# Writing the steps of TensorE into the program at their planned end

## The chip, the cores and the metric

The kernel runs on one core of a Trainium2 chip. The time is the device time of one execution in microseconds; of several runs the median is given. A profile is one execution with every instruction's begin and duration. Engines: PE is TensorE's matmuls, PEld its weight loads, DVE VectorE, ACT ScalarE, POOL GpSimd, SP the engine that issues the DMAs.

## What is computed

Window attention over 4 x 576 positions (8 heads of 64, each position sees itself and the 63 before it), then two feed-forward layers on the 2304 x 512 result, all in float32:

```python
def reference(**kwargs):
    attn_out = _attn_ref(**attn_kwargs)       # softmax(scale * q k^T, window of 64) v
    x = attn_out.transpose(0, 2, 1, 3).reshape(B * S, H * D)
    x = _moe_ref(x=x, **moe_kwargs)           # h = x @ w_in; g = s * relu(h)**2 + b; g @ w_out
    return _moe2_ref(x=x, **moe2_kwargs)      # h = x @ w_in; g = max(h,0) + alpha*min(h,0); g @ w_out
```

Both layers have w_in of 512 x 2048 and w_out of 2048 x 512.

## The kernel before

A matmul in full float32 precision is made of three matmuls of rounded parts (high x high, high x low, low x high), so each operand exists as a pair "h" and "l". Attention (function group) runs over five blocks of tokens, head pair by head pair; the first block is done in two groups of two head pairs each. The first two groups of hidden columns of layer 1 go straight through (hidden, project). The rest of layer 1 and layer 2 use Strassen's scheme with seven products in place of eight (hidden_pair): each call handles two hidden tiles of 128 columns and two halves of 384 tokens. In the last three groups of layer 2 the output side is done with seven products too (output).

In hidden_pair a product is six matmuls of 384 columns. Products 1, 2 go to a PSUM tile b1, products 5 and 4 to b4, and the sums that several outputs share to one tile "hb" of two PSUM banks (line 1661, 128 x 2 x 512 float32): products 6 and 3 to its first bank, product 7 to its second. Between them ACT copies partial sums from bank to bank (line 1027, in the trace always this line: ab<-h, aq<-h, ab<-ab, h<-ab), and VectorE adds the fourth part to both banks at the end (lines 1047, 1049). In the trace "hb" appears as "ab" and b1, b4 as "h"; the matmuls are line 1016. The lines are

```python
            product(7, 4, b3_, hb3, False)
            product(3, 5, b2_, hb2, False)
            copy(b4_, b3_, [hb3], [b4], 4)
            product(4, 6, b4_, b4, False)
```

(lines 1038 to 1041; b2_ is the first bank of "hb", b3_ the second). There are 39 such calls. The projections back to 512 columns are line 1507 (straight) and line 1299 (seven products); the planner puts them between products wherever they are ready. The last product 4 of the last call of output is made in two halves of 192 columns (line 1358), each with its own sum and its own DMA to the output.

Nothing of this is issued in the order of the listing. Every piece of work is a step of class Plan: ways (an engine, a planned cost in microseconds, the function that writes the instructions, a tail), the names it reads and writes, and a due time. step derives from the names which earlier steps it depends on; the two banks of "hb" are two names. emit is a list scheduler: it keeps for each engine when it is free, for each step when it is done, takes the step that can begin first (the one most due if several on that engine can), and calls its function at once. So instructions are written to the program in the order in which the planner begins them, for all engines alike, and the order of each engine is the order of its steps. The semaphore waits are made afterwards from that program: an instruction waits for those written before it on other engines that touch the same memory.

Of the kernel before, what the change touches and what calls it, by code (L numbers as in the profile page):

```python
# [2 lines left out]

# [79 lines left out]
class Plan:  # L83
# [100 lines left out]
    def emit(self):  # L184
        n = len(self.steps)
        after = [[] for _ in range(n)]
        for i, (_, deps, _, first, _) in enumerate(self.steps):
            for d in deps + first:
                after[d].append(i)
        path = [0.0] * n  # L190
        for i in range(n - 1, -1, -1):
            cost = min(w[1] + w[3] for w in self.steps[i][0])
            path[i] = cost + max((path[j] + 0.1 for j in after[i]), default=0.0)
        rank = [(-self.steps[i][2], path[i]) for i in range(n)]

        def hop(a, b):

            if a == b:
                return 0.0 if a == "pe" else 0.12
            return 0.2 if "pe" in (a, b) else 0.1  # L200

        took = {}
        left = [len(s[1]) + len(s[3]) for s in self.steps]
        done = [0.0] * n
        free = {"sp": 0.7, "dve": 2.2, "pool": 0.75, "act": 2.0, "pe": 1.1}
        pool_from = 0.0
        ready = {i for i in range(n) if left[i] == 0}
        order = []
        while ready:
            cands = []  # L210
            for i in ready:
                ways, deps, _, _, after_ = self.steps[i]
                best = None
                for w in ways:
                    share = len(w) > 4
                    w = w[:4]
                    t = max((done[d] + hop(took[d], w[0]) for d in deps), default=0.0)
                    t = max(t, free.get(w[0], 0.0), after_)
                    if w[0] == "pe" and t < self.SLOW:
                        w = (w[0], w[1] * 2, w[2], w[3])  # L220
                    if w[0] == "sp" and t < self.SLOW_DMA:
                        w = (w[0], w[1] * self.DMA_FACTOR, w[2], w[3])
                    if share:
                        w = (w[0], w[1] + 0.8 * max(0.0, min(free["pool"], t + w[1]) - max(t, pool_from)), w[2], w[3])
                    value = t + w[1] * (1.0 + self.SPARE[w[0]]) + w[3]
                    if best is None or value < best[0]:
                        best = (value, t, w)
                cands.append((best[1], i, best[2]))
            t0, i0, b0 = min(cands, key=lambda c: (c[0], self.steps[c[1]][2], c[1]))
            t0, i0, b0 = max(  # L230
                (c for c in cands if c[2][0] == b0[0] and c[0] <= t0 + self.WINDOW),
                key=lambda c: (rank[c[1]], -c[1]),
            )
            eng, cost, fn, tail = b0
            free[eng] = t0 + cost
            if eng == "pool":
                pool_from = t0
            done[i0] = t0 + cost + tail
            took[i0] = eng
            ready.remove(i0)  # L240
            order.append((t0, eng))
            fn()
            for j in after[i0]:
                left[j] -= 1
                if left[j] == 0:
                    ready.add(j)
        assert len(order) == n
        return max(done)


@with_exitstack
# [1528 lines left out]
```

## Time and profile before

| | |
|---|---|
| median of 3 runs | 842.01 us (841.2 to 842.93) |
| the profiled execution | 841.64 us |
| its span, first to last instruction | 839.6 us |
| granted TensorE clock, mean | 0.999 |
| PE busy | 821.4 us (98%) |
| PEld busy | 768.6 us (92%) |
| DVE busy | 702.6 us (84%) |
| ACT busy | 555.2 us (66%) |
| POOL busy | 105.4 us (13%) |
| DMA queue 1, share of 16 engines | 74.2% |

Busy times are unions of the instructions' spans. A row of a timeline merges neighbouring instructions of one line and kind: begin, duration of the whole run, engine, line, operation, written<-read, shapes, count; in brackets how long the engine stood idle before it and what ended that. A matmul's end is modelled and reaches over the begin of the next one, so what counts on PE is the distance between begins.

### The profile page before, as it was taken

The numbers are of one execution on the slowest core, as the hardware profiler recorded it, in microseconds if no ns is written. First come the engines' busy times: TensorE is split into PE (matmuls) and PEld (weight loads), VectorE is DVE, ScalarE is ACT, GpSimd is POOL, SyncE is SP. The second block draws the span as 40 slices with busy tenths as digits, with TensorE's granted clock in tenths as the row PEclk, the third lists the DMA queues.
The fourth block names the chain that finished last, engine by engine and source line by source line (L and its number), as shares of the span: only waits on it lengthen the run. The fifth ranks groups of instructions, "written<-read, shape, count | busy, mean of one in ns | idle before, by whom it ended". The sixth has DMA issues, their size and how long they took to land.

```text
span 839.6 us, 15049 instructions
## 1 busy us (share of the span) xinstructions
PE 821.4 (98%) x5481; PEld 768.6 (92%) x5485; DVE 702.6 (84%) x1195; ACT 555.2 (66%) x1249; POOL 105.4 (13%) x117
## 2 busy tenths in 40 slices
PE   7899999999999999999999999999999999999998
PEld 4688887888899999999999999999989999999998
DVE  6977899698995698789949898978799988888695
ACT  6777997644575576778748677775566566656461
POOL 6542355532100001001000000000000000000000
PEclk9999999999999999999999999999999999999999
DMA  8575976476648999989698676998785599469813
GB/s 284 185 231 153 283 229 197 164 261 242 236 170 324 368 342 368 405 311 369 249 388 300 259 314 246 333 363 304 278 301 187 211 328 346 131 212 350 319 47 114
DMA packets 81258, 224.61 MB, mean 268 GB/s; under 512 B 8096, under 2 KB 33824, under 8 KB 81184
## 3 DMA queue, kind: packets, MB, share of 16 engines
q1 hardware_dynamic: 81184, 223.65, 74.2%
q8 instruction: 43, 0.70, 0.3%
q14 instruction: 31, 0.25, 0.1%
HBM read 154.67 MB, written 68.94 MB: 266 GB/s over the span
## 4 chain that ended last, share of the span: by engine, by line
PE 69%; DVE 13%; DMA 12%; ACT 3%; issue 1%; POOL 1%; SPq 0%; DVEq 0%; ACTq 0%; POOLq 0%
PE y L1507 16%; PE h L1016 14%; PE y L1299 13%; PE ab L1016 11%; PE h L1417 7%; DMA raw<-w_out 4%; PE y L1477 3%; DMA raw<-w_in 3%; DMA vd<-al 2%; DVE raw L694 1%; PE ab L531 1%; PE y L636 1%; PE y L605 1%; DVE raw L699 1%; DVE raw L690 1%
## 5 line engine op out<-in xcount | busy, mean ns | idle before, releaser
L1016 PE MATMUL h<-ax,aw 128*128 128x384 f32 x936 | 184.4, 335 | 2.0 <-ACT h L1027 1.2
L1016 PEld LDWEIGHTS h<-ax,aw 128*128 128x128 f32 x936 | 163.9, 188 | 4.1 <-ACT h L1027 1.8
L1507 PE MATMUL y<-ax,woh 128*128 128x384 f32 x672 | 153.9, 335 | 2.3 <-DVE ay L1601 1.8
L1016 PE MATMUL ab<-ax,aw 128*128 128x384 f32 x702 | 139.9, 335 | 1.1 <-ACT ab L1027 0.6
L1016 PEld LDWEIGHTS ab<-ax,aw 128*128 128x128 f32 x702 | 122.9, 188 | 3.0 <-ACT ab L1027 1.6
L1507 PEld LDWEIGHTS y<-ax,woh 128*128 128x128 f32 x672 | 119.3, 188 | 4.2 <-DVE ay L1601 3.3
L1507 PE MATMUL y<-ax,wol 128*128 128x384 f32 x336 | 95.0, 334 | 0.0
L1417 PE MATMUL h<-ax,aw 128*128 128x512 f32 (+1 forms) x360 | 84.3, 377 | 0.8 <-DVE ax L654 0.7
L1417 PEld LDWEIGHTS h<-ax,aw 128*128 128x128 f32 x360 | 61.9, 189 | 12.4 <-DVE ax L654 1.6
L1299 PE MATMUL y<-ax,woh 128*128 128x384 f32 (+1 forms) x273 | 61.7, 333 | 0.0
L1507 PEld LDWEIGHTS y<-ax,wol 128*128 128x128 f32 x336 | 61.5, 188 | 0.0
L1128 ACT ACTIVATE al<-h 128x384 f32<-128x384 f32 (+2 forms) x58 | 30.1, 519 | 40.0 <-PE h L1417 21.6
L680 ACT ACTIVATE raw<-raw 128x512 f32<-128x512 f32 x56 | 37.5, 674 | 21.8 <-DMA raw<-w_in 14.2
L588 POOL TENSOR_TENSOR as__83<-as__83,den 128x512 f32<-128x512 f32 x36 | 41.5, 1173 | 59.9 <-DVE den L581 37.0
L1299 PEld LDWEIGHTS y<-ax,woh 128*128 128x128 f32 x273 | 48.4, 188 | 0.3 <-ACT y L1313 0.3
L1323 DVE TENSOR_TENSOR ay<-y,ay 128x384 f32<-128x384 f32 (+1 forms) x73 | 39.3, 546 | 10.5 <-PE y L1299 6.6
L764 POOL TENSOR_TENSOR al<-al,raw 128x512 f32<-128x512 f32 x15 | 21.8, 1450 | 193.4 <-DVE raw L699 193.4
L694 DVE SCALAR_TENSOR_TENSOR raw<-raw 128x512 int32<-128x512 int32 x56 | 42.9, 773 | 2.9 <-ACT raw L684 2.7
L1299 PE MATMUL y<-ag,wol 128*128 128x384 f32 x192 | 43.9, 335 | 0.4 <-DVE ag L711 0.4
L1313 ACT COPY y<-y 128x384 f32<-128x384 f32 x54 | 25.1, 465 | 27.7 <-PE y L1299 24.2
L1145 ACT ACTIVATE aq<-aq,slope 128x384 f32<-128x384 f32 x48 | 27.2, 610 | 23.9 <-DVE aq L1049 23.8
L570 ACT ACTIVATE as__83<-as__83,nm 128x128 f32<-128x128 f32 x96 | 37.3, 392 | 4.7 <-DVE nm L556 4.5
(189 smaller groups left out, 1670.9 us busy)
## 6 DMA issues: line engine op xcount, KB each, us to landing
ax<-xd SPq DMA_DIRECT2D x91, 768.0 KB, 6.8
aw<-wd SPq DMA_DIRECT2D x33, 512.0 KB, 5.3
xd<-ax SPq DMA_DIRECT2D x21, 768.0 KB, 4.1
raw<-w_in SPq DMA_DIRECT2D x28, 512.0 KB, 5.7
raw<-w_out SPq DMA_DIRECT2D x28, 512.0 KB, 5.6
wd<-ag SPq DMA_DIRECT2D x27, 512.0 KB, 5.0
xd<-aq SPq DMA_DIRECT2D x12, 768.0 KB, 4.2
xd<-ax SPq DMA_DIRECT2D x36, 192.0 KB, 4.7
```

Source lines behind the costliest of these rows:

```text
L570: nc.scalar.activation(sm3()[:, x, :], S_(h)[:, i * P:(i + 1) * P] if summed else sm3()[:, x, :], AF.Exp, bias=T[nm][:, x:x + 1], scale=sc ...
L588: eng.tensor_mul(x, x, d)
L680: [act(512, lambda: nc.scalar.activation(T[t], H().bitcast(F32), AF.Abs, scale=65536.0))],
L694: [dve(512, lambda: nc.vector.scalar_tensor_tensor(out=L(), in0=H(), scalar=-0x80000000, in1=L(), op0=ALU.bitwise_and, op1=ALU.bitwise_or) ...
L1016: nc.tensor.matmul(bank(), W[:, wj, a, kt * P:(kt + 1) * P], X[:, c, kt, :], start=start and kt == 0 and y == 0, stop=kt == 1 and y == 2, ...
L1128: T.step([act(n, lambda: nc.scalar.activation(rn(), hn(), AF.Relu)), dve(n, lambda: nc.vector.tensor_scalar_max(rn(), hn(), 0.0))], reads= ...
L1145: T.step([act(HALF, lambda: nc.scalar.activation(r2n(), hn(), AF.Identity, scale=slope[:, f:f + 1]))], reads=[hk, "side"], writes=[r2], at ...
L1299: nc.tensor.matmul(v(to)[:, c], W[:, s, a * P:(a + 1) * P], G[:, h, c], start=start and p == 0 and y == 0, stop=p == 1 and y == 2, skip_gr ...
L1323: [dve(e.stop - e.start, lambda: nc.vector.tensor_add(T[k][:, e], v(x)[:, e], T[k][:, e]))],
L1417: nc.tensor.matmul(T[ps][:, :n].rearrange("p (c t) -> p c t", t=P), T[w][:, k * P:(k + 1) * P], T[X(x, k)], start=st, stop=sp,)
L1477: nc.tensor.matmul(T[Y(m)][:, :n], T[w[a]][:, m * P:(m + 1) * P], T[gx[c]], start=(x == 0 and j == 0), stop=(x == len(fs) - 1 and j == 2),)
L1507: nc.tensor.matmul(ps, T[w][:, m * P:(m + 1) * P], T[x], start=(i == 0 and j == 0 and not carried(m, layer, g)), stop=(last and j == 2), s ...
```

## The change

emit no longer calls a step's function when it picks the step. It records the picks, and a new function, write, calls the functions in a second pass: a step's key is its planned begin, for a step of PE its planned begin plus its planned cost, that is its planned end. Among the steps whose dependencies are written, and whose predecessor on the same engine is written, the one with the smallest key comes next. The picks, their engines and each engine's order stay as they are; what differs is the place of PE's steps among those of the other engines.

```diff
             order.append((t0, eng))
-            fn()
+            picked.append((i0, b0))
...
+        self.write(picked, [t for t, _ in order], after)
         return max(done)
+
+    def write(self, picked, begins, after):
+
+        left = [len(s[1]) + len(s[3]) for s in self.steps]
+        then, last, way, key = {}, {}, {}, {}
+        for (i, b), t in zip(picked, begins):
+            way[i] = (t, b)
+            key[i] = t + b[1] if b[0] == "pe" else t
+            if b[0] in last:
+                then[last[b[0]]] = i
+                left[i] += 1
+            last[b[0]] = i
+        heap = [(key[i], i) for i in way if left[i] == 0]
+        heapq.heapify(heap)
+        count = 0
+        while heap:
+            _, i0 = heapq.heappop(heap)
+            t0, (eng, cost, fn, _) = way[i0]
+            count += 1
+            fn()
+            for j in after[i0] + ([then[i0]] if i0 in then else []):
+                left[j] -= 1
+                if left[j] == 0:
+                    heapq.heappush(heap, (key[j], j))
+        assert count == len(way)
```

## Rows read from the trace of the kernel before

**Rows 1.** The page's first section: busy us, share of the span, instructions.
```profile
PE 821.4 (98%) x5481; PEld 768.6 (92%) x5485; DVE 702.6 (84%) x1195; ACT 555.2 (66%) x1249; POOL 105.4 (13%) x117
```

**Rows 2.** The chain that ended last, share of the span by engine.
```profile
PE 69%; DVE 13%; DMA 12%; ACT 3%; issue 1%; POOL 1%; SPq 0%; DVEq 0%; ACTq 0%; POOLq 0%
```

**Rows 3.** Busy us of each engine from 235 us to the end.
```profile
235.00:840.00 605.00, 595.25 (x3405) 588.03 (x3403) 502.02 (x876) 388.35 (x756) 9.48 (x7) 1.00 0.78 285
```

**Rows 4.** Timeline of PE, 388 to 395 us.
```profile
388.66 1.20 PE L1016 MATMUL ab<-ax,aw 128*128 128x384 f32 x6
389.70 0.51 PE L1507 MATMUL y<-ax,woh 128*128 128x384 f32 x2
...
390.22 1.21 PE L1016 MATMUL ab<-ax,aw 128*128 128x384 f32 x6
391.98 1.31 PE L1016 MATMUL h<-ax,aw 128*128 128x384 f32 x6 [0.55 <-ACT h L1027]
393.12 0.51 PE L1507 MATMUL y<-ax,woh 128*128 128x384 f32 x2
...
394.29 0.61 PE L1507 MATMUL y<-ax,woh 128*128 128x384 f32 x2 [0.48 <-DVE ay L1601]
```

**Rows 5.** Timeline of ACT in the same stretch.
```profile
389.66 0.73 ACT L769 ACTIVATE woh<-raw,s_sb 128x512 fp32r<-128x512 f32 x1
391.46 0.46 ACT L1027 COPY h<-ab 128x384 f32<-128x384 f32 x1 [1.07 <-PE ab L1016]
```

**Rows 6.** Timelines of PE and of ACT, 437 to 443 us.
```profile
440.53 0.51 PE L1507 MATMUL y<-ax,woh 128*128 128x384 f32 x2
...
441.20 1.31 PE L1016 MATMUL ab<-ax,aw 128*128 128x384 f32 x6
...
440.67 0.48 ACT L1027 COPY h<-ab 128x384 f32<-128x384 f32 x1
```

**Rows 7.** Timelines of PE and of ACT, 372 to 377 us.
```profile
373.06 2.24 PE L1016 MATMUL ab<-ax,aw 128*128 128x384 f32 x12
...
375.33 0.46 ACT L1027 COPY h<-ab 128x384 f32<-128x384 f32 x1 [1.10 <-PE ab L1016]
```

**Rows 8.** Timeline of PE, 579 to 586 us.
```profile
580.48 2.25 PE L1016 MATMUL ab<-ax,aw 128*128 128x384 f32 x12
583.34 2.35 PE L1016 MATMUL h<-ax,aw 128*128 128x384 f32 x12 [0.61 <-ACT h L1027]
```

**Rows 9.** Timelines of PE and of ACT, 453 to 458 us.
```profile
454.35 2.24 PE L1016 MATMUL ab<-ax,aw 128*128 128x384 f32 x12
...
455.97 0.51 ACT L1500 COPY y<-ay 128x384 f32<-128x384 f32 x1
456.63 0.46 ACT L1027 COPY h<-ab 128x384 f32<-128x384 f32 x1 [0.15 <-PE ab L1016]
```

**Rows 10.** Timelines of PE and of DVE at the end, 834 to 840 us.
```profile
835.20 0.50 PE L1299 MATMUL y<-ax,woh 128*128 128x192 f32 x3
835.53 0.49 PE L1299 MATMUL y<-ax,wol 128*128 128x192 f32 x3
...
836.07 0.62 DVE L1323 TENSOR_TENSOR ay<-y,ay 128x192 f32<-128x192 f32 x2 [0.76 <-PE y L1299]
```

**Rows 11.** Timelines of PE, ACT and DVE, 619 to 630 us.
```profile
620.62 2.36 PE L1016 MATMUL ab<-ax,aw 128*128 128x384 f32 x12 [0.60 <-ACT ab L1027]
...
628.16 1.33 PE L1016 MATMUL ab<-ax,aw 128*128 128x384 f32 x6
...
622.25 0.62 ACT L731 CAST as__83<-al 128x512 fp32r<-128x512 f32 x1
...
624.48 0.95 DVE L1049 TENSOR_TENSOR aq<-ab,aq 128x768 f32<-128x768 f32 x1
```

**Rows 12.** Timelines of PE and of ACT, 15 to 33 us.
```profile
18.47 2.12 PE L636 MATMUL y<-ay 128*64 128x64 f32 x62 [0.35 <-ACT ay L612]
...
20.86 0.38 ACT L649 CAST ax<-y 128x256 fp32r<-128x256 f32 x1
```

More of the change, by code (lines that the diff above doesn't have):

```diff
@@ L1 @@
+import heapq
 import struct
@@ L208, in emit @@
         order = []
+        picked = []
         while ready:
```

## The prediction

> **What bounds the kernel now.** I read the page's first section, then the chain by engine, then PE's share of the stretch from 235 us on, then the timelines of PE and ACT around the Strassen products, and at last both ends of the span. TensorE is busy for 821.4 of 839.6 us [rows 1], and 69% of the chain that ended last is PE [rows 2]. From 235 us on PE stands idle for 605.00 - 595.25 = 9.75 us, of which some 3.6 lie behind its last matmul [rows 3, 10]. So a microsecond that PE waits is nearly a microsecond of the kernel, and little waiting is left to remove.
>
> **What the change can touch.** No instruction is added, and each engine keeps its order. What can move is who waits for whom where two engines use the same PSUM tile and no step's reads or writes order them: there the step that is written later waits. The rows show this in both directions on the tile "hb", whose two banks hold products 2 and 3 of a hidden pair. The last copy of a pair (line 1040, in the trace L1027 h<-ab) reads only the second bank, which product 7 filled; product 3 (line 1039) writes only the first. At 388.66 product 7 starts, three projection matmuls and product 3 (390.22) follow [rows 4]. ACT is free at 389.66 + 0.73 = 390.39, product 7 has been over since 389.86, yet the copy starts at 391.46, when product 3 is over as well: 1.07 us idle, put down to PE's ab [rows 5]. At 441.20 it is the other way: product 3, whose place in PE's row was 440.53 + 0.52 = 441.05 (three matmuls take half of the 1.04 of six), starts only when the copy of 440.67 is over (441.15) [rows 6]. A PE step was written at its planned begin, so a product 3 that follows product 7 closely was written ahead of the copy; with the change it is written at its end, 6 x (0.0137 + 384 x 0.000417) = 1.04 us later. I worked the planner's times through for the 39 pairs; they decide the order of writing alone, and none is taken as a time of the chip. In 28 pairs the copy stands first already. In the other 11 the planned begin of the copy lies 0.20 to 0.68 us behind that of product 3, so all 11 turn round: **product 3 will wait for the copy**.
>
> The Trainium skill, in "PSUM — Partial Sum Buffer", section "PSUM bank collisions raise a hardware error", says that pairs of engines on different banks ran clean, so the chip would need neither wait here. The trace agrees only that the program is stricter: by that rule the sum below would be 0, and the copy of 391.46 would have started at 390.39 [rows 5].
>
> **The price of one turned pair.** Six products take 389.70 - 388.66 = 1.04 us [rows 4]. A copy starts 0.20 us after the place where PE's next matmul would stand (391.46 against 390.22 + 1.04 = 391.26), takes 0.46, and PE resumes 0.06 later (391.98 against 391.92): 0.72 us [rows 4, 5]. The six matmuls behind that wait took 393.12 - 391.98 = 1.14 for 1.04, another 0.10. So 0.82 us where ACT is free.
>
> **The eleven.** In the plain case products 7 and 3 stand together as twelve ab matmuls from 373.06, ACT is free at 374.23 and waits 1.10 us for the last of them [rows 7]. Five are like that (product 3 due at 238.5, 374.1, 680.3, 769.0, 796.1), and today the projections behind product 3 hide the copy entirely; that cover is gone: 5 x 0.82 = +4.1. In two pairs PE already waits today, for product 4 needs the copy: at 391.98 (0.72 + 0.10 = 0.82 lost) [rows 4] and at 583.34 (due at 580.48 + 2.08 = 582.56: 0.78 + 0.10) [rows 8]. There the wait only moves from behind product 3 to ahead of it: gained 0.82 + 0.88, paid 390.39 + 0.46 + 0.06 - 390.22 + 0.10 = 0.79 and 0.82, so -0.1 together.
>
> In three pairs ACT is late. At 455.39 product 3 would be due, but ACT is busy until 455.97 + 0.51 = 456.48 [rows 9]: 1.09 + 0.46 + 0.06 = 1.61 (the restart's 0.10 goes against the 0.1 by which ACT's rows overlap). Two repeat the pattern, ACT free 0.89 us after product 3 is due: 1.41 each. Above: 1.61 + 1.41 + 1.41 = 4.43. Below: 3 x 0.82 = 2.46, if PE's delay by then lets ACT catch up. ACT's work ahead of these copies is part PE's (projections' sums), part the weights' (fed by DMA), so neither end is nearer; I take the middle, +3.45.
>
> The eleventh follows 620.62 [rows 11]. Product 3 is due at 621.66, ACT is free at 622.25 + 0.62 = 622.87: a stall of 1.73. But what comes later there is not PE's: its next product on hb starts at 628.16, while behind the stalled product 3 lie 24 matmuls, so PE would get there at 621.66 + 1.73 + 1.04 + 4.16 = 628.59. +0.43 (0 to 1.73), and the sum on VectorE that reads both banks started at 624.48 behind VectorE's own work, against 621.66 + 1.73 + 1.04 + 0.20 = 624.63, so it hardly moves.
>
> **Two turned waits elsewhere.** The last product 4 (line 1358) comes in two halves of one bank; today VectorE's add of the first half waits for the second half's matmuls (first half done at 835.20, add at 836.07) [rows 10]. Turned, the second half waits for the add: 0.20 + 0.31 (half of 0.62) + 0.06 + 0.10 = 0.67 later, while today's second add stands 0.31 behind the first and then no longer does. I take +0.43; 0.3 to 0.7. At the start, the second half of the second head group's values (line 631) will wait for ACT's cast of the first half, which starts at 20.86 although PE's run of values ends by 20.59 [rows 12]. PE would lose about 1.4 us, but it waits afterwards for other engines anyway: 0 to 0.8, I take 0.2.
>
> **What is swallowed.** A delayed PE finds other waits shorter: 0.48 at 394.29 [rows 4], 0.15 at 441.20 [rows 6]. Against 9.75 - 3.6 us of idle PE, of which the two waits that move are 1.7, between 0 and 2.0 seems fair; I take 0.7. No queue is moved past another: the DMAs keep SP's order, and POOL's steps touch no PSUM.
>
> **The sum**: 4.1 - 0.1 + 3.45 + 0.43 + 0.43 + 0.2 - 0.7 = +7.8 us. The profiled execution took 841.64 (span 839.6 and 2.0 around it), so 849.4; the median of the three runs, 842.01, lies 0.37 above it: **849.8 us**. Lower ends: 4.1 - 0.1 + 2.46 + 0 + 0.3 + 0 - 2.0 = +4.8, 846.8 on the median's basis. Upper ends: 4.1 - 0.1 + 4.43 + 1.73 + 0.7 + 0.8 = +11.7, 853.7.
>
> **Rivals.**
> 1. *The change moves no wait that matters.* The tile's banks would be told apart, or the copy's delay in rows 5 has another cause. Then 842, within 0.2%. Against it: both directions are seen [rows 5, 6], and the 0.06 us between copy and matmul recurs. Chance 0.08.
> 2. *Faster.* In the seven pairs with a free ACT the copy runs about 1.05 us earlier [rows 5, 7], and so does all that queues behind it on ACT, among it the preparation of weights on which PE waits later. If those waits shrink by more than the stalls cost, the end comes earlier. It decides from 7.8 us of swallowed waiting on; idle PE time before the tail is some 6 us, so at best about 840. Chance 0.05.
> 3. *Much slower.* PE's stalls meet a late ACT everywhere, as at 455.39 [rows 9]: 11 x 1.5 = 16.5, 858. Against it: in seven pairs ACT was idle for more than 1.0 us. Chance 0.05.
>
> **Chances.** The forecast holds 0.82. A measurement of this kernel tells about 0.2% (1.7 us) from no change. Faster 0.05, same 0.08, slower 0.87. The range runs from a little under the lower ends to the upper ends, 845.5 to 854.0, and leaves the rivals and some of the forecast's rim out.
>
> **What would show it.** In the profile after, copies L1027 h<-ab that follow twelve ab matmuls should be gone: six ab, a hole of some 0.7 us, the copy in it, then six ab. In the list of waits "PE ab L1016 <- ACT h L1027", 0.2 us once, should rise to some 6 us in about ten waits, and ACT's wait for PE's ab ahead of this copy should fall by about 1 us in each. PE's idle time from 235 us on should grow by about as much as the span. I am wrong if product 3 still follows product 7 at once, if PE's sums of idle time stay, or if PE stalls but the weights' waits behind vanish by the same amount.

## The result, and the profile after

The changed kernel took 849.04 us (median of 5 runs, 848.86 to 851.97), the kernel before 841.2 us in the runs beside it (median of 5, 840.64 to 842.93). The ratio is 1.0098, with a 95% interval of 1.0078 to 1.0118: slower by 0.8 to 1.2%. The profiled execution of the changed kernel took 849.01 us, its span is 847.2 us against 839.6 (7.5 us more before rounding). One run of the kernel before, beside the experiments, took 1636.23 us and is left out of every figure below. All lines of the code lie 28 further down: the products are L1044, the copies L1055, the projections L1535 and L1327, VectorE's sums of projections L1629 and L1351.

The page's first section and the chain by engine, which answer to [rows 1, 2]:

```profile
PE 823.7 (97%) x5485; PEld 769.1 (91%) x5485; DVE 703.5 (83%) x1195; ACT 555.5 (66%) x1249; POOL 105.0 (12%) x117
...
PE 72%; DVE 13%; DMA 7%; ACT 5%; issue 2%; POOL 1%; SPq 0%; ACTq 0%; DVEq 0%; POOLq 0%
```

No engine has more instructions to run (a few PE records are missing in the trace before); the differences in busy time are below 2.5 us. What has changed is who waits. From the list of waits between 235 and 850 us (engine, line, waited for: us in total, times, longest):

```profile
ACT h L1055 <- PE ab L1044: 13.9, 21, 1.5
...
PE ab L1044 <- ACT h L1055: 7.8, 11, 1.3
```

In the kernel before the same two lines are:

```profile
ACT h L1027 <- PE ab L1016: 21.9, 28, 1.7
...
PE ab L1016 <- ACT h L1027: 0.2, 1, 0.2
```

ACT waits 8 us less, which is worth little because ACT is not the bound. PE waits 7.6 us more for this copy, in eleven places, and there the loss arises. That this number nearly equals the growth of the span is chance: two of the eleven waits replace PE's 1.2 us ahead of product 4, and several other terms, below, add to the sum or take from it. The busy time from 235 us on (length of the stretch, then PE, PEld, DVE, ACT and POOL) answers to [rows 3]:

```profile
235.00:847.20 612.20, 597.48 (x3408) 588.63 (x3407) 503.08 (x877) 389.07 (x758) 9.75 (x8) 1.00 0.77 282
```

The window of [rows 3] runs to 840.00, 0.4 us past the last instruction, which counts as idle there. With that taken off, the stretch has grown by 7.5 us and PE's idle part by 5.3 (from 9.4 to 14.7). The other 2.2 us are counted as busy: a run of six matmuls takes 1.04 us between begins but is shown 1.20 long, so a hole begins some 0.17 us late in the record, and the slower matmuls behind it (0.10 to 0.14) are no hole at all. The eight new holes of the plain and the late pairs (table below) cost 7.9 us and are shown as 5.6.

One turned pair, at its place in [rows 7]. PE, then ACT, 375 to 379 us:

```profile
375.32 1.20 PE L1044 MATMUL ab<-ax,aw 128*128 128x384 f32 x6
377.07 1.34 PE L1044 MATMUL ab<-ax,aw 128*128 128x384 f32 x6 [0.55 <-ACT h L1055]
378.25 0.51 PE L1535 MATMUL y<-ax,woh 128*128 128x384 f32 x2
...
376.56 0.46 ACT L1055 COPY h<-ab 128x384 f32<-128x384 f32 x1
```

The twelve matmuls in a row have become six and six. Product 7 is over at 375.32 + 1.04 = 376.36, the copy starts 0.20 later, takes 0.46, PE resumes 0.05 after it, and product 3 takes 378.25 - 377.07 = 1.18 in place of 1.04: 0.71 + 0.14 = 0.85 us.

To find where the loss arises I set the begin of each matmul after against the begin of the same matmul before, and noted every place where the difference steps:

| place (us in the kernel before) | step, us (PE later: +) |
|---|---|
| start, values (19.90), what is left by 41 us | +0.72 |
| five plain pairs: 238.52, 374.10, 680.29, 769.03, 796.07 | +0.85, +0.85, +0.89, +0.89, +0.89 |
| two replaced waits: 390.22 and 391.98, 581.52 and 583.34 | +0.73 - 0.81, +0.88 - 0.87 |
| three pairs with a late ACT: 407.77, 455.39, 533.62 | +0.89, +1.63, +1.10 |
| the pair at 620.62, with all that follows until 627 | -0.88 + 1.41 - 0.18 - 0.69 = -0.34 |
| VectorE's sum waited for at 326.69; smaller steps at 254 | +0.73; +0.4 |
| other waits that shrank: 277, 343, 394, 441 to 447, 535, 552, 573, 718, 767 | -2.2 |
| small drifts between these places | -0.1 |
| tail, from the first half's begin to the last sum's end | +0.44 |

### The profile page after: what moved, and what is told of

It is laid out like the page before. It is cut to its first block, busy times and chain, and to the rows that moved or that the text cites. A ratio compares the mean times of both kernels' runs of the same rounds, so it can differ in the third digit from the quotient of the medians.

```text
span 847.2 us, 15061 instructions
## 1 busy us (share of the span) xinstructions
PE 823.7 (97%) x5485; PEld 769.1 (91%) x5485; DVE 703.5 (83%) x1195; ACT 555.5 (66%) x1249; POOL 105.0 (12%) x117
## 4 chain that ended last, share of the span: by engine, by line
PE 72%; DVE 13%; DMA 7%; ACT 5%; issue 2%; POOL 1%; SPq 0%; ACTq 0%; DVEq 0%; POOLq 0%
PE y L1535 18%; PE h L1044 15%; PE y L1327 14%; PE ab L1044 11%; PE h L1445 7%; PE y L1505 3%; DMA raw<-w_out 2%; DVE raw L722 1%; DMA raw<-w_in 1%; PE y L664 1%; PE ab L559 1%; DVE raw L718 1%; PE y L633 1%; DVE raw L717 1%; DMA al<-w_in 1%
## 5 line engine op out<-in xcount | busy, mean ns | idle before, releaser
L1044 PE MATMUL h<-ax,aw 128*128 128x384 f32 x936 | 184.2, 335 | 0.7 <-DVE raw L1176 0.4
L1044 PEld LDWEIGHTS h<-ax,aw 128*128 128x128 f32 x936 | 164.0, 188 | 2.2 <-DVE raw L1176 1.1
L1535 PE MATMUL y<-ax,woh 128*128 128x384 f32 x672 | 153.9, 335 | 2.5 <-DVE ay L1629 2.3
L1044 PE MATMUL ab<-ax,aw 128*128 128x384 f32 x702 | 142.3, 337 | 7.9 <-ACT h L1055 7.8
L1044 PEld LDWEIGHTS ab<-ax,aw 128*128 128x128 f32 x702 | 122.7, 188 | 12.3 <-ACT h L1055 11.7
L1535 PEld LDWEIGHTS y<-ax,woh 128*128 128x128 f32 x672 | 119.5, 188 | 4.1 <-DVE ay L1629 3.8
L1535 PE MATMUL y<-ax,wol 128*128 128x384 f32 x336 | 95.0, 335 | 0.0
L1327 PE MATMUL y<-ax,woh 128*128 128x384 f32 (+1 forms) x273 | 61.7, 333 | 0.5 <-DVE ay L1351 0.5
L1535 PEld LDWEIGHTS y<-ax,wol 128*128 128x128 f32 x336 | 61.6, 188 | 0.0
L1351 DVE TENSOR_TENSOR ay<-y,ay 128x384 f32<-128x384 f32 (+1 forms) x73 | 39.6, 549 | 11.8 <-PE y L1327 7.1
L1327 PEld LDWEIGHTS y<-ax,woh 128*128 128x128 f32 x273 | 48.4, 188 | 0.7 <-DVE ay L1351 0.6
L1327 PE MATMUL y<-ag,wol 128*128 128x384 f32 x192 | 43.6, 335 | 0.0
```

Of the source, the lines that this page charges most:

```text
L1044: nc.tensor.matmul(bank(), W[:, wj, a, kt * P:(kt + 1) * P], X[:, c, kt, :], start=start and kt == 0 and y == 0, stop=kt == 1 and y == 2, ...
L1327: nc.tensor.matmul(v(to)[:, c], W[:, s, a * P:(a + 1) * P], G[:, h, c], start=start and p == 0 and y == 0, stop=p == 1 and y == 2, skip_gr ...
L1351: [dve(e.stop - e.start, lambda: nc.vector.tensor_add(T[k][:, e], v(x)[:, e], T[k][:, e]))],
L1535: nc.tensor.matmul(ps, T[w][:, m * P:(m + 1) * P], T[x], start=(i == 0 and j == 0 and not carried(m, layer, g)), stop=(last and j == 2), s ...
```

## The experiments

The theory: eleven times product 3 waits for a copy which reads the tile's other bank, because the copy now stands ahead of it in the program and the tile is ordered as one piece. The rivals are named with each run. Each kernel is compared with the kernel before on the same chip: the first four share one set of its runs (median 843.1 us), the others a second (841.49).

**Only product 3 is written late**, that is at its planned end.

```
-            key[i] = t + b[1] if b[0] == "pe" else t
+            key[i] = t + b[1] if i in self.thirds else t
...
+                if j == 3:
+                    T.thirds.add(i)
```

> Only product 3 of the hidden pairs is written at its planned end, every other step at its planned begin. Theory (eleven turned copies make the loss): eleven waits of PE's ab for the copy, about 7.5 us in sum, PE's starts as in the changed kernel between 235 and 830 us but without the steps at the start (+0.7) and the tail (+0.7): +5.8 to +7.0 us against before, ratio 1.007 to 1.0083. Rival A (the loss is made by all other steps of PE that are written later, the copies only being where it shows): 0 to +1.5 us.

Measured: 849.88 us (849.26 to 850.96), ratio 1.0082 (1.0053 to 1.0112), +6.9 us. 39 of PE's steps account for the whole loss, within the interval; rival A falls.

**All but product 3 are written late.** The same edit with `if b[0] == "pe" and i not in self.thirds`.

> The reverse: every step of PE is written at its planned end but product 3 of the hidden pairs, which stays at its planned begin. Theory: no copy turns, PE waits for the copy 0.2 us in all as before; what is left is the wait of the values at the start (0 to 0.8 us) and that of the last product 4's second half (0.3 to 0.7 us): +0.3 to +1.5 us against before, ratio 1.0004 to 1.0018. Rival A: +6 us or more, 1.007.

Measured: 842.2 us, ratio 0.9996 (0.9974 to 1.0018), no difference that can be told; the value lies a little under the 1.0004 to 1.0018 expected, the interval takes them in. PE's waits for the copy from 235 us on, first in this kernel, then in the one above:

```profile
PE ab L1045 <- ACT h L1058: 0.2, 1, 0.2
```

```profile
PE ab L1045 <- ACT h L1058: 9.4, 14, 1.3
```

Three of those 14 waits (at 296.06, 343.29 and 441.20 in the kernel before) belong to pairs whose copy was written first already.

The trace of the kernel with all but product 3 written late shows both of the other turned waits. At the start PE is 0.87 us later than before by 25 us and still 0.72 later at 235 us. Between 276 and 280 us it gains 1.2 us, but that does not show the start's delay swallowed: the version with two tiles written at the planned begin (below), where PE is not late but 0.4 us early at 276 us, gains the same 1.2 us there. The tail costs its 0.43 us (below). Neither can be seen in the median.

**The tile in two.** The banks become two tiles of one bank each (from a pool of their own), and VectorE's sum over both becomes two operations.

```
-            b2_, b3_ = (lambda: T["hb"][:, 0, :HALF]), (lambda: T["hb"][:, 1, :HALF])
+            b2_, b3_ = (lambda: T["hb", 0][:, :HALF]), (lambda: T["hb", 1][:, :HALF])
...
-                    nc.vector.tensor_add(x2(T[both]), x, y)
+                for x, half in ((b3_, slice(HALF, C)), (b2_, slice(0, HALF))):
+                    out = T[both][:, half]
...
+                        nc.vector.tensor_add(out, x(), T[p5])
```

Written at the planned end:

> The changed kernel with the two banks of hb as two tiles of one bank each; VectorE's total, one operation over 768 columns of both banks, becomes two over 384 columns (39 operations more on VectorE, some 0.1 to 0.2 us each). Theory (the wait exists only because one tile is ordered as one piece): neither product 3 nor the copy waits for the other, PE's waits for the copy go from 7.8 us to what product 4 behind it needs; the start and the tail stay (+0.7 and +0.7), the two waits of before at 391.98 and 583.34 (0.8 us each) go: -2 to +2 us against before plus what VectorE's extra operations bring to the path, below 4 us in all. Rival B (the two banks collide on the chip or the copy is needed by product 3 for another reason): +6 to +9 us, as the changed kernel.

Measured: 839.9 us, ratio 0.9966 (0.9944 to 0.9989). The rest of the change is still there, and the loss is gone: rival B falls. The pair of [rows 4, 5] in this kernel, PE and then ACT:

```profile
389.60 1.20 PE L1045 MATMUL hb<-ax,aw 128*128 128x384 f32 x6
...
391.16 1.20 PE L1045 MATMUL hb<-ax,aw 128*128 128x384 f32 x6
392.20 1.20 PE L1045 MATMUL h<-ax,aw 128*128 128x384 f32 x6
...
391.24 0.48 ACT L1056 COPY h<-hb 128x384 f32<-128x384 f32 x1
```

The copy (391.24 to 391.72) runs while product 3 writes the neighbouring bank, and product 3 takes 392.20 - 391.16 = 1.04 us, its usual time. Neither engine waits for or slows the other, and product 4 follows at once. The two waits of the kernel before [rows 4, 8] are gone as well.

The same, written at the planned begin:

> The same two tiles, with every step written at its planned begin. Theory: with the tile split the place of writing matters only at the start and the tail, so this lies 0.5 to 1.5 us below split_end; against before -3 to +2 us. Rival B: within 0.5 us of before, and 7 us below split_end.

Measured: 839.74 us, ratio 0.9962 (0.9943 to 0.9981), within the expectation against before. With the tile split the place of writing is worth 0.2 us between medians, where 0.5 to 1.5 were expected; the runs of one kernel scatter by more than that (838.1 to 841.19 here, 838.25 to 845.09 at the planned end), so this decides nothing about the start and the tail. **This version beats both kernels**: 0.4% under the kernel before, about 1.3% under the changed one (0.9962 / 1.0098). VectorE's total costs hardly more: 1.01 us for both halves against 0.96 for the one operation (at 375 us).

**Five plain pairs alone.** As in the first experiment, for the five pairs whose ACT was idle.

```
+FIVE = ((0, 2, 0, 0), (0, 4, 0, 0), (1, 2, 1, 0), (1, 3, 1, 0), (1, 3, 0, 0))
...
+                if j == 3 and (layer, g, q, p) in FIVE:
+                    T.thirds.add(i)
```

> Product 3 is written at its planned end in five pairs only, those where ACT stood idle and projections followed product 3 (due at 238.5, 374.1, 680.3, 769.0 and 796.1 us); all else at its planned begin. Theory: 5 x 0.82 = 4.1 us of stalls, less 0.5 to 1 swallowed: +3.0 to +4.1 us against before, ratio 1.0036 to 1.0049. Rival C (single stalls are taken up by slack behind them, and the loss comes from the late-ACT pairs): below +1.5 us.

Measured: 846.95 us, ratio 1.0066 (1.0042 to 1.0089), +5.5 us: rival C falls, but the value lies above mine. The five steps themselves are the same as in the changed kernel, +0.85 to +0.89, 4.4 in sum for 4.1 expected. More than nothing was added elsewhere: +0.92 at 296.06, +0.45 at 326.69, +0.58 at 678.21, +0.46 at 717.91 and +0.36 at 766.67, against 1.9 us of waits that shrank. The largest of these, PE and then ACT:

```profile
296.66 1.32 PE L1046 MATMUL ab<-ax,aw 128*128 128x384 f32 x6 [0.64 <-ACT h L1059]
...
295.57 0.67 ACT L710 ACTIVATE raw<-raw 128x512 f32<-128x512 f32 x1 [2.12 <-DMA raw<-w_in]
296.14 0.47 ACT L1059 COPY h<-ab 128x384 f32<-128x384 f32 x1
```

In this pair the copy was written ahead of product 3 already. It stands in ACT's queue behind an operation on weights that waited 2.12 us for its DMA (0.43 in the kernel before). In the ten profiles that wait lies between 0.38 and 2.12 us, and the queue of the DMAs takes 100% of the 16 engines from 280 to 296 us in the kernel before. VectorE's sum that PE waits for at 326.69 lies between 1.18 and 2.19 us, likewise. How much of these two the delay of PE causes and how much differs from one execution to the next was not separated; together they move one profile by about 1 us either way.

**The copy twice, written late.** In the eleven pairs ACT runs the copy two times.

```
+                    for _ in range(times):
+                        nc.scalar.copy(out(), src())
...
-            copy(b4_, b3_, [hb3], [b4], 4)
+            copy(b4_, b3_, [hb3], [b4], 4, 2 if (layer, g, q, p) in ELEVEN else 1)
```

> The changed kernel, with ACT's copy h<-ab run twice in a row in the eleven turned pairs (one further copy of 0.46 us in each). Theory (PE's product 3 waits for this copy and for nothing else): each of these stalls grows by 0.46 us, 11 x 0.46 = 5.1, less 1 to 2 swallowed: +3 to +5 us against the changed kernel, +10.5 to +13 against before, ratio 1.0125 to 1.0155. Rival D (PE waits there for something else that happens to end with the copy): within 1 us of the changed kernel, 1.0085 to 1.011.

Measured: 858.01 us (855.97 to 859.17), ratio 1.0188 (1.0155 to 1.0222). Rival D falls; the size is beyond the theory's upper end. PE's waits for the copy rose from 7.8 us to 14.0, in the same eleven places, so the eleven stalls grew by 6.2 us in sum (5.1 expected): by 0.5 in eight of them, by 0.7 to 0.9 in three where ACT came late. Some 2 us of other waits shrank. The profiled execution, 7.0 us longer than the changed kernel's, also shows the clock fall, behind the two longest waits for the copy (2.22 and 1.85 us). PE at the first of them, and the busy time with the granted clock (the sixth number after the length) there and at the second:

```profile
457.68 1.21 PE L1048 MATMUL ab<-ax,aw 128*128 128x384 f32 x6
461.10 1.89 PE L1048 MATMUL ab<-ax,aw 128*128 128x384 f32 x6 [2.22 <-ACT h L1060]
462.79 0.84 PE L1543 MATMUL y<-ax,woh 128*128 128x384 f32 x2
```

```profile
458.00:462.00 4.00, 1.78 (x10) 1.46 (x9) 3.13 (x5) 3.97 (x10) 0.00 (x0) 0.95 1.03 344
462.00:463.00 1.00, 1.00 (x5) 1.00 (x4) 0.00 (x0) 0.94 (x2) 0.00 (x0) 0.50 0.87 287
463.00:465.00 2.00, 2.00 (x7) 2.00 (x7) 1.87 (x3) 0.88 (x2) 0.00 (x0) 0.50 0.93 381
465.00:470.00 5.00, 5.00 (x30) 5.00 (x30) 4.22 (x7) 2.89 (x5) 0.00 (x0) 1.00 0.87 351
...
632.00:636.00 4.00, 4.00 (x16) 4.00 (x15) 3.01 (x5) 1.81 (x4) 0.00 (x0) 0.57 0.68 216
```

The clock falls from its upper level (2.4 GHz, 1.00) to its lower one (1.2 GHz, 0.50), and matmuls stand 0.32 us apart in place of 0.17. PE falls back another 1.5 us at the first place and 1.6 at the second: 3.1 us that the theory lacked.

**The copy twice, written at the planned begin.**

> The same doubled copies in the same eleven pairs, with every step written at its planned begin, as before. Theory: the copies lie behind product 3, covered by projections in nine pairs; only ahead of product 4 at 391.98 and 583.34 do they lengthen PE's wait: 2 x 0.46 = +0.9 us, +0.4 to +1.8 against before, ratio 1.0005 to 1.0021. Rival E (ACT's extra time itself costs, wherever it stands): as much as in twice_end, +3 to +5 us.

Measured: 844.33 us, ratio 1.0036 (1.0019 to 1.0052), +3.0 us (+1.6 to +4.4); expected were +0.4 to +1.8. The two places of the theory show +0.51 at 391.98 and +0.50 at 583.34, 1.0 in sum as forecast (0.9). The rest is PE waiting for ACT elsewhere (+0.44 at 441.20, +0.50 at 535.83, +0.65 at 628.16) and slower matmuls behind some of the doubled copies (+0.49 at 240.6, less at some more places), against some 2 us of waits that shrank. So 5 us of work on an engine that is busy for two thirds of the span cost some 2 us even behind the cover of projections. Rival E holds for this part, but the same work cost about three times as much in the kernel where PE waits for it (858.01 - 849.04 = 9 us, the clock's part among them).

**PE written 3 us early.**

```
-            key[i] = t + b[1] if b[0] == "pe" else t
+            key[i] = t - 3.0 if b[0] == "pe" else t
```

> The other direction: PE's steps are written 3.0 us ahead of their planned begin, all others at their planned begin, so product 3 stands ahead of the copy in nearly all 39 pairs and the copy waits for it. Theory: where projections follow product 3 this costs nothing; where product 4 follows it directly (some 13 pairs beside the two of before) PE waits behind product 3 for the delayed copy, 0.82 us each, 10.7 in all less 1 to 3 swallowed: +7 to +11 us against before, ratio 1.008 to 1.013, with PE's waits now at h<-ax,aw and not at ab. Rival F (earlier is always better, the loss is a matter of late writing): -2 to +1 us.

Measured: 860.96 us, ratio 1.0231 (1.0194 to 1.0268), far above the 7 to 11 us expected; rival F falls. The form is as forecast, the wait now stands ahead of product 4 (PE, and the list of waits over the whole span):

```profile
249.91 1.31 PE L1044 MATMUL h<-ax,aw 128*128 128x384 f32 x6 [0.61 <-ACT h L1055]
```

```profile
ACT h L1055 <- PE ab L1044: 88.3, 36, 6.0
...
PE h L1044 <- ACT h L1055: 8.1, 14, 0.6
...
PE y L1535 <- ACT ay L1615: 2.0, 2, 1.6
PE y L1327 <- ACT y L1341: 1.7, 3, 1.1
```

Two of the fourteen waits are those of the kernel before; the twelve new ones cost 10.3 us with the slower matmuls behind them (10.7 forecast). What I left out is ACT's queue: its copies wait 88.3 us for PE's ab (21.9 in the kernel before), and sums of projections stand behind them, for which PE then waits too (+1.89 at 566.55, +1.40 at 659.49). These and ten smaller steps come to 9.6 us, against some 2 us of waits that shrank; no run tried that cause by itself. Writing earlier is no cure; here it is the dearer side.

## Why the prediction held

849.8 us were forecast, 849.04 measured.

**The mechanism** is the one forecast: no instruction more, all eleven pairs turned, and the loss gone when the tile is two tiles. The eleven waits sum to 7.8 us where some 6 were named; ACT's waits for PE's ab fell by 8.0 us, about 1 in each of the seven pairs whose ACT was free. PE's idle time grew by 5.3 and not by the whole 7.5, since I forgot that the record of a matmul reaches into the hole behind it. Of the 9.75 us of idle time that it started from, 0.4 lie past the end of the span; no term of the sum hangs on that.

**The price of one turned pair**, 0.82 us, measured 0.85 to 0.89. Taking its parts from the two directions in which the kernel before already waited [rows 4 to 6] carried the whole forecast: the five plain pairs came to +4.4 (4.1), the two replaced ones to -0.1 (-0.1).

**The three pairs with a late ACT** came to 3.6 (3.45; between 2.46 and 4.43), but not evenly: 1.63 for 1.61, 1.10 for 1.41, 0.89 for 1.41. The two that fell short show why. In the kernel before, ACT waited for a DMA of weights on its way to each of these copies (0.49 us at 407.77, 0.57 at 533.62), and so it did at the pair at 620.62:

```profile
405.83 0.68 ACT L680 ACTIVATE raw<-raw 128x512 f32<-128x512 f32 x1 [0.49 <-DMA raw<-w_out]
...
532.33 0.69 ACT L680 ACTIVATE raw<-raw 128x512 f32<-128x512 f32 x1 [0.57 <-DMA raw<-w_out]
...
618.96 0.67 ACT L680 ACTIVATE al<-al 128x512 f32<-128x512 f32 x1 [2.81 <-DMA al<-w_in]
```

After, it waits for no DMA at the first, 0.24 us at the second and 0.71 at the third:

```profile
407.63 0.49 ACT L1156 ACTIVATE al<-h 128x384 f32<-128x384 f32 x1 [0.58 <-PE h L1044]
408.01 0.67 ACT L708 ACTIVATE raw<-raw 128x512 f32<-128x512 f32 x1
...
410.75 0.46 ACT L1055 COPY h<-ab 128x384 f32<-128x384 f32 x1
...
536.84 0.68 ACT L708 ACTIVATE raw<-raw 128x512 f32<-128x512 f32 x1 [0.24 <-DMA raw<-w_out]
...
621.98 0.68 ACT L708 ACTIVATE al<-al 128x512 f32<-128x512 f32 x1 [0.71 <-DMA al<-w_in]
```

PE was 2.8 us later at the first, the weights had arrived, and ACT's run up to the copy lost its wait: 1.41 - 0.49 = 0.92 for 0.89 measured, 1.41 - (0.57 - 0.24) = 1.08 for 1.10. At 455.39 ACT was packed without a wait and stayed as late as before. The kernel with product 3 alone written late repeats it: there ACT waits 0.22 and 0.33 us for the two DMAs, which makes 1.41 - 0.27 = 1.14 and 1.41 - 0.24 = 1.17, and the steps are 1.16 and 1.17 (1.62 at 455.39). The prediction said that neither end was nearer; what decides was to be read from [rows 9] and their like, by whether ACT's queue ahead of the copy holds a wait for a DMA.

**The pair at 620.62** was mis-sized: +0.43 (0 to 1.73) forecast, -0.34 measured. The stall is there (+1.41), and what comes later was indeed not PE's; but PE's own wait ahead of the pair, 0.60 in [rows 11], vanished for the reason just given, ACT's shorter wait for its DMA (0.71 us and not 2.81). I had counted no gain from it in this term.

**The start** gave +0.72 where I took 0.2, inside 0 to 0.8; it is still +0.71 at 235 us, and how much of it reaches the end is not shown. **The tail** is exact. First half's begin to the end of VectorE's last sum was 834.55 to 836.69 (836.07 + 0.62, [rows 10]), 2.14 us, and is 841.92 to 844.50, 2.58: +0.44 for +0.43.

```profile
841.92 0.47 PE L1327 MATMUL y<-ax,woh 128*128 128x192 f32 x3
842.23 0.50 PE L1327 MATMUL y<-ax,wol 128*128 128x192 f32 x3
843.19 0.58 PE L1327 MATMUL y<-ax,woh 128*128 128x192 f32 x3 [0.45 <-DVE ay L1351]
...
844.14 0.36 DVE L1351 TENSOR_TENSOR ay<-y,ay 128x192 f32<-128x192 f32 x1 [1.01 <-PE y L1327]
```

**What is swallowed** was 2.2 us, above the upper end of 2.0 that I took (0.7 was the value); how much of it is PE's delay and how much one execution against another was not separated. It did not show in the sum because a term was missing on the other side: waits that grew, +0.73 at 326.69 and some +0.4 at 254. The first is VectorE's: its work on the weights stood 2.4 us later than before when PE stood 1.7 later, so that the sum which PE waits for came 0.7 later still. That PE's delay caused this is not shown: the same wait is 1.80 us (1.35 before) in the version with two tiles written at the planned begin, where PE stood 1.6 us earlier than before.

```profile
329.12 0.62 PE L1535 MATMUL y<-ax,woh 128*128 128x384 f32 x2 [2.10 <-DVE ay L1629]
...
328.52 1.01 DVE L1629 TENSOR_TENSOR ay<-y,ay 128x384 f32<-128x384 f32 x2
```

So the total, +7.8 forecast and +7.5 in the profiles, is closer than its terms, and that closeness is luck: 0.5, 0.3 and 0.15 too little at the start, the plain pairs and the late pairs, 1.1 of grown waits left out, 0.8 too much at 620.62, 1.5 too little swallowed.

**The rivals.** That no wait moves is refuted by the list of waits. That ACT's earlier copies pay for it: they did run earlier, and 2.2 us of other waits shrank, under a quarter of what was lost; whether they shrank for that reason was not tried. That PE meets a late ACT everywhere: only three of eleven pairs, and two of them were less late than they looked.

On the rule of the Trainium skill that the prediction weighed, "PSUM — Partial Sum Buffer", section "PSUM bank collisions raise a hardware error": the runs with two tiles now show what the page states for different banks, with ACT reading one for 0.48 us inside the 1.04 us in which PE writes the other. The loss came from how the program was ordered, not from the banks.

## What to carry to other kernels

Where waits are made from the order in which instructions are written, the place of writing is a decision of its own: for each pair of steps that share a tile but no data, read which one stands first, and price both sides from a place where the kernel already waits in that direction. If neither needs the other, give each its own tile, which ends the question; here that was worth more than any order of writing. And before a late engine's lateness is added to a new stall, look whether its queue holds a wait for a DMA: that part does not slide with the delay.

## What the runs showed of the chip

- The clock fell from 1.00 to 0.50 behind waits of PE of 1.80 to 2.22 us and was back after 3 to 4 us, at a price of about 1.5 us at each of the two places of the copy run twice. It did not do so behind every wait of that length: behind 2.10 us at 329.12 in the changed kernel and behind 2.19 in the first experiment it stayed at 1.00, as it did behind the longest wait for the copy there (1.33 us). In the versions with two tiles it fell as well, behind a wait which the kernel before has too (1.35 us): 1.86 us long when written at the planned end, 1.80 at the planned begin:

```profile
325.62 0.83 PE L1537 MATMUL y<-ax,woh 128*128 128x384 f32 x2 [1.80 <-DVE ay L1631]
```

```profile
325.60:328.50 2.90, 2.88 (x10) 2.88 (x11) 1.75 (x4) 0.72 (x1) 0.00 (x0) 0.54 1.01 417
```

- This is part of why single executions differ: in the runs of the kernel before, a mean clock of 1.000 went with 839.25 to 843.0 us, one of 0.994 with 849.84. What made the clock fall in one execution and not in the next was not tried.
